# A fused sparse-attention and feed-forward kernel: the order of its side steps laid out anew

## The chip, the cores and the metric

The kernel runs on one core of a Trainium2 chip. The metric is device time in microseconds of one execution; a run is a whole execution, and the median of the runs shown is the time that counts. One further execution was profiled; its trace is what is read here. TensorE (PE, with its weight loads PEld) multiplies; VectorE (DVE), ScalarE (ACT) and GpSimd (POOL) do the rest; SyncE (SP) and ScalarE issue transfers. Each engine goes through its own list in order.

## What is computed

Attention for 8 batches, 8 heads, 576 tokens and 64 features a head: heads 0 to 3 see the last 32 tokens, heads 4 to 7 every 32nd token. Its output, 4608 tokens of 512 features, goes through a feed-forward layer with a hidden width of 2048.

```python
scores = scale * np.matmul(q, k.transpose(0, 1, 3, 2))
scores = np.where(masks[None, :, :, :], scores, -1000000000.0)
scores = scores - np.max(scores, axis=-1, keepdims=True)
attn = np.exp(scores)
attn = attn / (np.sum(attn, axis=-1, keepdims=True) + 1e-09)
attn_out = np.matmul(attn, v)
...
h = x @ w_in
g = np.where(pos, h, np.where(neg, 0.0, (h + beta) ** 2 / (4.0 * beta)))   # pos: h >= 1, neg: h <= -1
out = g @ w_out
```

## The kernel before

Tokens go through the feed-forward in columns of 512. The weights and activations are split into a high and a low half, and each product of 128x128 by 512 columns stands for one of three pairs of halves (high-high, high-low, low-high, in this order).

The first three chunks of 512 tokens are plain ("classic"): for each of 16 slices f of the hidden width, `up(c, f)` is 12 products into one of two PSUM banks, a gate on ScalarE and VectorE and a rounding to two halves follow, and `down` two slices later is 12 products, in two parts of six. The last 3072 tokens are three chunks of 1024, each computed with seven products of half-size blocks in place of eight: an up part of 56 units of six products (`up_block`, L988) and a down part of 28 units of 12 (`down_block`, L1039). A unit of the down part waits for two factors that SP fetches from DRAM into a ring of seven.

Beside the products stand the steps. All of them are written into tables, each with a position, and are issued in the order of positions. A position counts TensorE's chunks: six products are one position. The first chunk runs from -64 to 0 (slice f at -64 + 4f), the second from 0 to 64, the third from 64 to 128, and each of the large chunks takes 112 from 128 on. A step at a position is put into the program before the first TensorE chunk that is issued after that position: in the classic chunks there are three such places a slice (after `up`, between the two parts of `down`, after `down`), in the large chunks one after each unit. On TensorE this says where a step stands among the products; on another engine it says only which step comes before which. Semaphores do the rest.

```python
def until(t):
    while agenda and agenda[0][0] < t:
        _, _, do, what = agenda.pop(0)
        do(*what)
...
todo = [(GATE[c > 0], lambda: gate(c, f)), (ROUNDED[c > 0], lambda: pend.append((c, f, rounded(c, f))))]
if c or f > 1:
    gs = pend.pop(0)
    todo += [(2, lambda: down(*gs, (0, 1))), (3, lambda: down(*gs, (2, 3)))]
for at, do in sorted(todo, key=lambda x: x[0]):
    until(t + at)
    do()
until(t + 4)
```

The tables:

- `WORK[b]`: the attention of batch b, a letter and a unit 0 to 3 (units 0 and 1 are the local heads, 2 and 3 the strided). On TensorE: `s` scores (L544), `f` transposes (L671), `v` values and `V1` those of units 1 and 3 (L734). On VectorE: `m` mask (L604), `x` maximum (L630), `b` subtraction, `q` sum (L645), `w` reciprocal and product (L658), `t` transpose (L695), `l` low half (L810; it issues nothing for tokens from column 1536 on, which are kept whole). On ScalarE: `e` exponential, `p` sum plus epsilon, `h` copy of the values out of PSUM (L801). On POOL: `a` subtraction (L634); `r` is a reciprocal on VectorE (L657) and a product on POOL (L658). On SP: `j`, `J` a trip through DRAM, `Q`, `F`, `P` loads. Scores, transposes and values of the batches share two PSUM banks, so that a block waits until the step that reads the block before it out is done; from batch 5 on `s1`, `s3` and `v2` use two others.
- `CONV`: the conversion of weight slice f, half i (`E5.0` is the last step for up(0,5), `E5.1` for down(0,5)): `A`, `L` (L404, L408) and `D` (L425) on ScalarE, `B` (L412) and `E` (L429) on VectorE, `C` (L416) on POOL. `E` makes the low half.
- `SUMS`: sums of weight slices (POOL, ScalarE, VectorE, and a store on ScalarE's queue); `SHIP`: stores of weight slices to DRAM, on ScalarE's queue.
- `X_WORK`, `U_WORK`, `G_WORK`: sums, gates and splits of the large chunks; in `U_WORK`, `a111` adds a product's result to a block on VectorE (L964); in `G_WORK`, `r40` or `r30` takes a result out (L1020 on ScalarE, L1022 on VectorE) and SP stores it (L881).

The opening, up to the second slice of the first chunk, is an order of its own (`BEGIN`) and isn't touched.

Of the kernel before, what the change touches and what calls it, by code (L numbers as in the profile page):

```python
# [35 lines left out]
WORK = {1: [(-60.38, 's0'), (-55.74, 'm0'), (-55.4, 'x0'), (-52.6, 'a0'), (-51.93, 's1'), (-51.84, 'Q2 Q3'), (-51.74, 'e0 q0'),  # L36
# [196 lines left out]
def tile_sparse_attention_then_ffn(  # L233
# [843 lines left out]
    with tc.manual_schedule():  # L1077
# [25 lines left out]
        def sum_step(n, step):  # L1103
            s, half_ = SUMS[n][0]
            i, j = divmod(n, NP)
# [106 lines left out]
```

## Time and profile before

| | |
|---|---|
| median of 3 runs | 817.14 us (817.0 to 818.74) |
| profiled execution, its own time | 816.39 us |
| its span, first to last instruction | 814.6 us |
| TensorE busy | 803.3 us, 99% |
| VectorE busy | 572.1 us, 70% |
| ScalarE busy | 494.2 us, 61% |
| POOL busy | 242.3 us, 30% |
| granted TensorE clock | 1.0 of full speed throughout |

Busy times are unions of the instructions' spans. The share of TensorE leaves some 11 us of the span in which it does nothing, part of them before its first instruction and after its last.

### The profile page before, as it was taken

Reading aid. Unit: us, or ns where it says so; the run is one execution under the profiler, and the core shown is the slowest. Engines: PE = TensorE matmul, PEld = TensorE weight load, DVE = VectorE, ACT = ScalarE, POOL = GpSimd, SP = SyncE. Lnnn points to the kernel's source line nnn. Section 1 sums busy time; section 2 is a strip of 40 time slices with the busy share of each in tenths; the row PEclk is TensorE's granted clock in tenths of the full one; section 3 lists DMA queues with packets and bytes.
Section 4 is the critical chain, followed back from the end, with each engine's and each line's share of the span. In section 5 each row is a group of like instructions: output and inputs, shape, how many; then the busy total and the mean of one; then the engine's idle time right before and its main releaser. Section 6 shows DMA issues by size and latency. Waiting matters only on the chain.

```text
span 814.6 us, 17829 instructions
## 1 busy us (share of the span) xinstructions
PE 803.3 (99%) x6969; PEld 655.9 (81%) x6969; DVE 572.1 (70%) x845; ACT 494.2 (61%) x868; POOL 242.3 (30%) x229
## 2 busy tenths in 40 slices
PE   8999999999999999999999999999999999999997
PEld 6778888888878888887888888788888888888885
DVE  5998868767548547775698877765678733777672
ACT  5888855545355446577764464677745545885442
POOL 5454544873347520421134101230310000114000
PEclk9999999999999999999999999999999999999999
DMA  9935437788868775998888977897666776666764
GB/s 347 408 137 198 156 111 274 267 299 278 271 222 293 257 242 180 330 292 255 261 295 252 285 260 239 270 282 226 178 201 205 246 223 193 194 195 188 219 205 147
DMA packets 101795, 195.10 MB, mean 239 GB/s; under 512 B 17104, under 2 KB 32464, under 8 KB 99664
## 3 DMA queue, kind: packets, MB, share of 16 engines
q1 hardware_dynamic: 92496, 164.60, 63.6%
q10 hardware_dynamic: 9216, 29.36, 9.3%
q8 instruction: 55, 0.90, 0.4%
q14 instruction: 28, 0.23, 0.1%
HBM read 147.26 MB, written 46.66 MB: 238 GB/s over the span
## 4 chain that ended last, share of the span: by engine, by line
PE 95%; DMA 2%; issue 1%; DVE 0%; ACT 0%; POOL 0%; SPq 0%; ACTq 0%; POOLq 0%; DVEq 0%
PE yo L1039 16%; PE o L891 16%; PE y L988 16%; PE h L846 16%; PE zo L1039 8%; PE z L988 8%; PE x L988 4%; PE xo L1039 4%; PE xp L734 4%; PE sc L544 3%; DMA qk<-in_qk_s 2%; DMA v<-in_v_s 0%; PE tp L671 0%; POOL pr L634 0%; SPq L479 0%
## 5 line engine op out<-in xcount | busy, mean ns | idle before, releaser
L988 PE MATMUL y<-x,wr 128*128 128x512 f32 x576 | 141.6, 392 | 0.1
L846 PE MATMUL h<-xq,w 128*128 128x512 f32 x576 | 139.7, 391 | 0.5 <-DVE w L429 0.5
L1039 PE MATMUL yo<-hl,wr 128*128 128x512 f32 x576 | 133.1, 390 | 0.0
L891 PE MATMUL o<-gh,w 128*128 128x512 f32 x384 | 130.1, 399 | 0.0
L846 PEld LDWEIGHTS h<-xq,w 128*128 128x128 f32 x576 | 107.5, 188 | 23.6 <-DVE w L429 0.9
L988 PEld LDWEIGHTS y<-x,wr 128*128 128x128 f32 x576 | 107.1, 188 | 24.0 <-DVE gb L964 0.6
L1039 PEld LDWEIGHTS yo<-hl,wr 128*128 128x128 f32 x576 | 107.9, 188 | 22.6 <-DVE hl L943 0.3
L891 PEld LDWEIGHTS o<-gh,w 128*128 128x128 f32 x384 | 72.1, 188 | 16.1
L891 PE MATMUL o<-gl,w 128*128 128x512 f32 x192 | 75.0, 391 | 0.0
L988 PE MATMUL z<-x,wr 128*128 128x512 f32 x288 | 73.3, 390 | 0.0
L971 POOL TENSOR_TENSOR ga<-gb,ga 128x1024 f32<-128x1024 f32 x9 | 22.0, 2449 | 156.8 <-DVE ga L856 122.3
L634 POOL TENSOR_TENSOR pr<-pr,st 128x384 f32<-128x384 f32 (+3 forms) x22 | 29.2, 1326 | 132.8 <-DVE st L630 132.2
L1039 PE MATMUL zo<-hl,wr 128*128 128x512 f32 x288 | 66.1, 390 | 0.0
L943 DVE TENSOR_TENSOR hl<-ga,hl 128x1024 fp32r<-128x1024 f32 x36 | 50.0, 1391 | 21.2 <-ACT hl L942 20.2
L457 POOL TENSOR_TENSOR xs<-w 128x512 f32<-128x512 f32 x32 | 44.7, 1416 | 63.5 <-DMA ks<-xs 25.8
L988 PEld LDWEIGHTS z<-x,wr 128*128 128x128 f32 x288 | 54.0, 188 | 11.5 <-ACT gb L962 0.3
L1039 PEld LDWEIGHTS zo<-hl,wr 128*128 128x128 f32 x288 | 54.0, 188 | 11.2
L853 ACT ACTIVATE tmp<-tmp 128x512 f32<-128x512 f32 x96 | 60.7, 633 | 3.0
L942 ACT CAST hl<-ga 128x1024 fp32r<-128x1024 f32 x36 | 37.8, 1053 | 39.2 <-PE yo L1039 15.7
L856 DVE SCALAR_TENSOR_TENSOR h<-h,u 128x512 f32<-128x512 f32 x47 | 32.7, 696 | 39.4 <-ACT u L853 39.0
L459 POOL TENSOR_TENSOR xs<-xs 128x256 f32<-128x256 f32 x64 | 52.3, 818 | 5.0
L850 ACT ACTIVATE u<-h,half 128x512 f32<-128x512 f32 x48 | 33.0, 688 | 32.5 <-PE h L846 26.9
(118 smaller groups left out, 1320.0 us busy)
## 6 DMA issues: line engine op xcount, KB each, us to landing
wr<-ks SPq DMA_DIRECT2D x192, 256.0 KB, 3.8
wr<-kq SPq DMA_DIRECT2D x144, 256.0 KB, 3.5
ks<-xs ACTq DMA_DIRECT2D x16, 1024.0 KB, 5.0
raw<-in_w SPq DMA_DIRECT2D x30, 512.0 KB, 9.5
kq<-w ACTq DMA_DIRECT2D x48, 256.0 KB, 3.7
qk<-in_qk_s SPq DMA_DIRECT2D x16, 604.0 KB, 5.9
qk<-in_qk_l SPq DMA_DIRECT2D x16, 576.0 KB, 5.7
v<-in_v_l SPq DMA_DIRECT2D x21, 384.0 KB, 5.7
```

The lines of the kernel that those rows point to most:

```text
L457: nc.gpsimd.tensor_tensor(out=b[:, :, f] if i else b[:, f], in0=hi, in1=lo, op=ALU.add)
L459: nc.gpsimd.tensor_tensor(out=st[:, to, HF:], in0=st[:, x, HF:], in1=st[:, y, HF:], op=op)
L734: nc.tensor.matmul(xp[p][j * D:(j + 1) * D, n], loaded[b, local, b0 + n][keys, j], qs, start=True, stop=True)
L846: nc.tensor.matmul(o_ps[c, f], wt[f][:, 0, h, x, e:e + P], xq[c][:, y, cc], start=first and n == 0, stop=last and n == len(todo) - 1)
L850: nc.scalar.activation(u, h, AF.Relu, bias=half, scale=0.5)
L853: nc.scalar.activation(u, u, AF.Square)
L856: nc.vector.scalar_tensor_tensor(out=to, in0=h, scalar=1.0, in1=u, op0=ALU.max, op1=ALU.min)
L891: nc.tensor.matmul(o_ps[c][d], wt[f][:, 1, h, x, e:e + P], gs[y], start=f == 0 and n == 0, stop=f == NF - 1 and n == 2)
L942: nc.scalar.copy(t[:, 0], src)
L943: nc.vector.tensor_tensor(out=t[:, 1], in0=src, in1=t[:, 0].bitcast(F32), op=ALU.subtract)
L988: nc.tensor.matmul(banks_of[s, q, j], w_[:, a, c * P:(c + 1) * P], xc[m][:, b, c], start=m in (1, 2, 5) and c + i == 0, stop=c == 1 and i ...
L1039: nc.tensor.matmul(to, w_[jj][:, a, d * P:(d + 1) * P], t[:, b, jj], start=m in (1, 2, 5) and k + jj + q == 0, stop=k == NP // 2 - 1 and j ...
```

## The change

All seven tables are replaced; nothing else is. The old and the new tables hold the same steps on the same engines, at other positions, but for five entries that are left out (`l1` of batch 2, `l0` to `l3` of batch 3). Entries that stood together at one position ('Q2 Q3', 'e0 q0') stand alone now. Positions up to -56 are the same. Over all kinds of steps the mean of the moves lies between some 4 positions earlier and 2.3 later; single steps move by up to 57 positions (a `SHIP`), most by one to three. The core of the diff, with the lines that hold the steps named below:

```diff
--- before.py
+++ after.py
@@ -33,200 +33,202 @@
...
-WORK = {1: [(-60.38, 's0'), (-55.74, 'm0'), (-55.4, 'x0'), (-52.6, 'a0'), (-51.93, 's1'), (-51.84, 'Q2 Q3'), (-51.74, 'e0 q0'),
-     (-51.61, 'p0'), (-51.49, 'm1'), (-51.2, 'x1'), (-51.12, 'a1'), (-50.21, 'r0'), (-47.65, 'e1'), (-47.64, 'q1'),
-     (-47.42, 'p1'), (-46.21, 'w1'), (-43.77, 'f0'), (-43.76, 'd0'), (-39.64, 's2'), (-39.4, 'm2 x2'), (-39.15, 'a2'),
-     (-35.94, 'v0'), (-35.84, 'F2'), (-35.81, 'e2'), (-35.73, 'q2'), (-35.57, 'h0 l0'), (-35.39, 'p2'), (-35.14, 'w2'),
...
-     (28.85, 'k3 r3'), (28.89, 'j2'), (29.15, 'J2'), (37.36, 'v2'), (37.46, 't3'), (37.87, 'h2'), (38.0, 'l2'),
-     (38.81, 'j3'), (41.17, 'J3'), (41.32, 'F4'), (44.62, 'V1'), (45.06, 'h1'), (45.32, 'l1'), (46.1, 'h3'),
-     (46.78, 'l3')],
- 3: [(26.83, 'Q0 Q1'), (29.08, 's0'), (37.27, 'm0'), (37.65, 'x0'), (37.85, 'b0'), (39.59, 'e0'), (40.48, 's1'),
...
-     (59.22, 'F2'), (59.61, 'h0'), (59.9, 'l0'), (59.93, 'x3'), (60.67, 't2'), (61.19, 'j2'), (61.5, 'F3 a3'),
...
-     (71.38, 'h2'), (72.41, 'F4'), (72.61, 'j3'), (73.19, 'l2'), (75.79, 'J3'), (82.43, 'V1'), (82.61, 'h1'),
-     (83.08, 'l1'), (83.16, 'h3'), (89.51, 'l3')],
...
-     (159.74, 'j3'), (163.55, 'v2'), (163.58, 'v0'), (163.89, 'F2'), (163.96, 'h0'), (164.19, 'F4'), (165.84, 'J3'),
...
-     (206.47, 't3'), (206.57, 'j3'), (209.86, 'F2'), (210.31, 'F4'), (210.71, 'h0'), (214.02, 'J3'), (218.14, 'v2'),
-     (218.76, 'V1'), (219.91, 'h2'), (219.92, 'h3'), (222.97, 'h1')],
...
-     (250.0, 's2'), (250.07, 's3'), (250.6, 'F3'), (250.87, 'm2'), (251.05, 'x2'), (251.16, 'p1'), (251.38, 'w1'),
...
-SUMS = [((0, 0), 30.03, 34.27, 34.91, 37.39), ((1, 1), 64.0, 67.03, 67.68, 74.53), ((0, 0), 16.76, 22.19, 23.74, 27.21),
...
- ((0, 0), 9.8, 15.48, 15.83, 16.18), ((1, 0), 73.17, 74.86, 75.67, 80.37), ((1, 1), 120.48, 122.48, 123.07, 124.52),
...
-X_WORK = {0: [(115.78, 2), (116.82, -7), (116.86, 1), (117.06, -6), (118.89, -4), (121.4, 7), (121.65, 4), (124.38, -5), (127.97, 5),
-     (128.22, 3), (128.79, 6)],
...
+WORK = {1: [(-60.38, 's0'), (-55.91, 'm0'), (-55.76, 'x0'), (-53.32, 'a0'), (-51.97, 'e0'), (-51.96, 'q0'), (-51.47, 's1'),
+     (-51.36, 'm1'), (-51.34, 'p0'), (-50.76, 'x1'), (-50.67, 'a1'), (-48.41, 'Q2'), (-47.84, 'r0'), (-44.93, 'e1'),
+     (-44.33, 'q1'), (-42.98, 'f0'), (-42.41, 'd0'), (-42.39, 'Q3'), (-42.29, 'p1'), (-41.64, 'w1'), (-38.33, 's2'),
+     (-37.48, 'm2'), (-37.45, 'x2'), (-35.84, 'a2'), (-35.7, 'v0'), (-35.68, 'h0'), (-35.6, 'e2'), (-35.37, 'F2'),
...
+     (36.92, 'J2'), (37.23, 'j3'), (37.38, 'v2'), (37.5, 'F4'), (38.57, 'J3'), (41.16, 'h2'), (41.35, 'l2'),
+     (44.18, 'V1'), (44.27, 'h1'), (45.93, 'h3'), (46.32, 'l3')],
+ 3: [(20.68, 'Q0'), (20.81, 'Q1'), (33.83, 's0'), (34.87, 'm0'), (34.99, 'x0'), (35.17, 'b0'), (39.66, 'e0'),
...
+     (161.1, 'j3'), (163.15, 'v2'), (163.36, 'h2'), (163.65, 'v0'), (163.95, 'F2'), (164.03, 'F4'), (164.28, 'h0'),
...
+     (208.37, 'r3'), (208.82, 'h0'), (209.24, 'F4'), (209.6, 't3'), (211.22, 'j3'), (212.22, 'v2'), (213.76, 'J3'),
+     (217.43, 'h2'), (219.15, 'V1'), (219.45, 'h3'), (230.78, 'h1')],
...
+     (255.23, 'w1'), (255.27, 't1'), (255.28, 'j1'), (255.3, 'a2'), (255.38, 'm3'), (256.09, 'e2'), (257.07, 'x3'),
...
+SUMS = [((0, 0), 30.98, 34.91, 35.07, 35.23), ((1, 1), 68.97, 69.39, 69.64, 74.86), ((0, 0), 20.69, 22.48, 22.88, 24.84),
...
+ ((0, 0), 7.28, 16.02, 16.64, 17.61), ((1, 0), 75.37, 76.25, 76.45, 78.18), ((1, 1), 115.03, 120.59, 122.35, 122.43),
...
+X_WORK = {0: [(101.78, 2), (110.78, 1), (118.17, -7), (118.33, -6), (121.1, -4), (123.64, 6), (123.89, 7), (129.32, -5), (129.48, 5),
+     (130.33, 3), (130.78, 4)],
...
 CONV = [(-63.99, 'L0.1'), (-63.97, 'A0.1 B0.1'), (-63.52, 'A1.1'), (-63.03, 'C0.1'), (-62.58, 'A3.0'), (-62.43, 'D0.1'),
...
- (-51.25, 'D3.1'), (-50.93, 'A4.1'), (-50.92, 'D5.0'), (-50.23, 'E3.1'), (-50.1, 'L4.1'), (-48.56, 'A6.0'),
- (-48.52, 'A5.1'), (-48.35, 'E5.0'), (-48.16, 'B4.1'), (-47.95, 'B6.0'), (-47.76, 'L6.0'), (-47.49, 'C4.1'),
- (-47.41, 'C6.0'), (-47.32, 'D4.1'), (-47.0, 'D6.0'), (-46.02, 'B5.1'), (-45.33, 'E6.0'), (-45.2, 'A7.0'),
...
- (-40.36, 'B7.1'), (-40.04, 'B8.0'), (-40.0, 'E7.0'), (-39.97, 'C7.1'), (-39.68, 'A6.1'), (-39.52, 'B6.1'),
- (-39.43, 'C8.0'), (-39.38, 'L6.1 C6.1'), (-39.09, 'D8.0'), (-38.69, 'A9.0'), (-38.65, 'L8.1'), (-38.44, 'E5.1'),
...
-     (456.33, 's43'), (461.13, 'r31'), (462.11, 'r41'), (462.46, 'r40'), (462.86, 'r30')]}
...
-     (249.85, 'n110'), (251.85, 'c111'), (252.05, 'a111'), (253.16, 'a011'), (254.14, 'n000'), (254.8, 'a001'),
...
-SHIP = [[1.27, 12.82, 7.42, 20.53, 13.61, 18.54, 30.97, 29.74, 34.32, 31.23, 40.56, 58.58, 43.6, 47.29, 57.58, 63.72],
- [67.18, 66.59, 57.74, 75.26, 81.54, 83.67, 104.23, 102.07, 98.47, 104.8, 100.58, 117.35, 100.49, 112.74, 129.16, 115.04]]
...
+ (-55.32, 'A4.1'), (-55.2, 'L5.0'), (-55.18, 'C4.0'), (-55.11, 'D2.1'), (-55.04, 'A5.0'), (-53.89, 'B5.0'),
...
+ (-51.62, 'C3.1'), (-50.95, 'C5.0'), (-50.81, 'L7.0'), (-49.52, 'D5.0'), (-49.22, 'L4.1'), (-49.17, 'E5.0'),
+ (-49.12, 'A5.1'), (-48.6, 'B5.1'), (-48.43, 'D3.1'), (-48.27, 'E3.1'), (-47.37, 'B4.1'), (-47.08, 'A6.0'),
+ (-46.92, 'B6.0'), (-46.8, 'L6.0'), (-46.78, 'C6.0'), (-46.52, 'A6.1'), (-46.47, 'C4.1'), (-45.48, 'L7.1'),
...
+ (-40.1, 'D7.0'), (-40.04, 'B6.1'), (-40.01, 'E7.0'), (-39.22, 'C6.1'), (-39.0, 'D6.1'), (-38.87, 'D5.1'),
+ (-38.57, 'C8.0'), (-37.88, 'D8.0'), (-36.66, 'E5.1'), (-36.58, 'E6.1'), (-36.5, 'E8.0'), (-36.47, 'C7.1'),
...
+     (458.33, 'r30'), (459.48, 's42'), (460.23, 's43'), (463.1, 'r40'), (463.12, 'r41')]}
...
+     (250.14, 'a001'), (250.83, 'f100'), (250.84, 'n100'), (251.23, 'c111'), (251.56, 'a111'), (251.84, 'f111'),
...
+SHIP = [[3.6, 1.13, -1.06, 29.51, 16.74, 37.99, 36.33, 16.76, -22.29, 32.1, 44.04, 93.57, 29.6, 34.85, 70.16, 53.52],
+ [80.62, 41.72, 52.33, 89.6, 79.44, 84.1, 109.2, 107.22, 99.77, 113.42, 99.29, 122.61, 66.19, 118.4, 121.29, 96.06]]
...
```

## Rows read from the trace of the kernel before

**Rows 1.** The page: busy us (share of the span) xinstructions; the chain by engine.
```profile
PE 803.3 (99%) x6969; PEld 655.9 (81%) x6969; DVE 572.1 (70%) x845; ACT 494.2 (61%) x868; POOL 242.3 (30%) x229
...
PE 95%; DMA 2%; issue 1%; DVE 0%; ACT 0%; POOL 0%; SPq 0%; ACTq 0%; POOLq 0%; DVEq 0%
```

**Rows 2.** The chain in order of time: start us, us, what.
```profile
754.97 21.76 PE yo L1039 x96
```

**Rows 3.** ScalarE's timeline, 38.5 to 45.5 us: start, us, instruction.
```profile
38.80 0.69 ACT L425 CAST w<-raw 128x512 fp32r<-128x512 f32 x1 [0.22 <-POOL raw L416]
...
42.97 0.66 ACT L850 ACTIVATE u<-h,half 128x512 f32<-128x512 f32 x1
```

**Rows 4.** TensorE's timeline at three blocks of values, and the next product.
```profile
177.66 1.28 PE L734 MATMUL xp<-pT,v 54*64 54x64 f32 x48
178.87 0.50 PE L891 MATMUL o<-gh,w 128*128 128x512 f32 x1
...
231.85 0.93 PE L734 MATMUL xp<-pT,v 54*64 54x64 f32 x48
232.71 1.66 PE L846 MATMUL h<-xq,w 128*128 128x512 f32 x6
...
391.89 1.51 PE L734 MATMUL xp<-pT,v 64*64 64x32 f32 x88
393.34 0.96 PE L988 MATMUL y<-x,wr 128*128 128x512 f32 x3
...
465.81 2.30 PE L734 MATMUL xp<-pT,v 54*64 54x64 f32 x136
468.04 1.20 PE L1039 MATMUL zo<-hl,wr 128*128 128x512 f32 x4
```

**Rows 5.** SP's timeline at the end.
```profile
810.92 0.41 SPq L881 DMA_DIRECT2D out<-kept  x1
```

**Rows 6.** Timelines around 517 and at 53.7 us; line L412 (min/median/max ns).
```profile
516.86 1.52 PE L988 MATMUL z<-x,wr 128*128 128x512 f32 x6
518.51 1.66 PE L988 MATMUL y<-x,wr 128*128 128x512 f32 x6
...
516.22 1.64 DVE L658 TENSOR_TENSOR pr<-pr,st 128x384 f32<-128x384 f32 x1
...
516.17 1.27 POOL L634 TENSOR_TENSOR pr<-pr,st 128x648 f32<-128x648 f32 x1 [2.46 <-DVE st L630]
...
53.69 0.56 DVE L658 TENSOR_TENSOR pr<-pr,st 128x384 f32<-128x384 f32 x1
...
L412 DVE TENSOR_SCALAR raw<-raw x34: 290/420/1694, 15.3 to 108.4; 128x512 uint32<-128x512 uint32 x30, 128x256 uint32<-128x256 uint32 x4
```

**Rows 7.** Timelines of TensorE, VectorE and POOL, 47 to 53 us.
```profile
48.12 0.67 PE L846 MATMUL h<-xq,w 128*128 128x512 f32 x2
49.28 2.57 PE L846 MATMUL h<-xq,w 128*128 128x512 f32 x10 [0.50 <-DVE w L429]
...
51.47 0.80 PEld L671 LDWEIGHTS tp<-ident,pr 128*128 128x128 f32 x6
...
48.47 0.22 DVE L657 RECIPROCAL st<-st 128x12 f32<-128x12 f32 x1
...
48.83 1.73 POOL L658 TENSOR_TENSOR pr<-pr,st 128x768 f32<-128x768 f32 x1 [1.33 <-DVE st L657]
```

**Rows 8.** Timelines of VectorE and TensorE, 63 to 68 us.
```profile
64.28 0.68 DVE L429 TENSOR_TENSOR w<-raw,w 128x512 fp32r<-128x512 f32 x1
...
66.31 0.39 PE L891 MATMUL o<-gl,w 128*128 128x512 f32 x1
```

**Rows 9.** TensorE's timeline, 377 to 382 us; the page's queue of instructions (packets, MB).
```profile
377.88 2.06 PE L734 MATMUL xp<-pT,v 54*64 54x64 f32 x126
381.67 0.53 PE L734 MATMUL xp<-pT,v 64*64 64x32 f32 x18 [1.72 <-issue]
...
q8 instruction: 55, 0.90, 0.4%
```

More of the change, by code (lines that the diff above doesn't have):

```diff
@@ L34 @@
 """
-WORK = {1: [(-60.38, 's0'), (-55.74, 'm0'), (-55.4, 'x0'), (-52.6, 'a0'), (-51.93, 's1'), (-51.84, 'Q2 Q3'), (-51.74, 'e0 q0'),
[60 rows of a table removed]
-SUMS = [((0, 0), 30.03, 34.27, 34.91, 37.39), ((1, 1), 64.0, 67.03, 67.68, 74.53), ((0, 0), 16.76, 22.19, 23.74, 27.21),
[5 rows of a table removed]
-X_WORK = {0: [(115.78, 2), (116.82, -7), (116.86, 1), (117.06, -6), (118.89, -4), (121.4, 7), (121.65, 4), (124.38, -5), (127.97, 5),
-     (128.22, 3), (128.79, 6)],
- 1: [(209.29, 2), (219.97, -7), (227.35, 7), (227.46, 1), (233.2, -6), (233.37, -5), (234.98, 5), (236.4, -4), (236.56, 3),
-     (237.47, 6), (242.51, 4)],
- 2: [(299.32, 1), (314.83, -7), (323.8, 7), (337.11, -6), (338.91, 6), (343.56, 2), (346.68, 3), (349.06, -4), (352.84, -5),
-     (353.14, 5), (355.46, 4)]}
+WORK = {1: [(-60.38, 's0'), (-55.91, 'm0'), (-55.76, 'x0'), (-53.32, 'a0'), (-51.97, 'e0'), (-51.96, 'q0'), (-51.47, 's1'),
[62 rows of a table added]
+SUMS = [((0, 0), 30.98, 34.91, 35.07, 35.23), ((1, 1), 68.97, 69.39, 69.64, 74.86), ((0, 0), 20.69, 22.48, 22.88, 24.84),
[5 rows of a table added]
+X_WORK = {0: [(101.78, 2), (110.78, 1), (118.17, -7), (118.33, -6), (121.1, -4), (123.64, 6), (123.89, 7), (129.32, -5), (129.48, 5),
+     (130.33, 3), (130.78, 4)],
+ 1: [(205.79, 2), (224.98, -7), (227.85, 1), (230.24, 3), (230.48, -6), (231.26, 7), (233.63, -5), (234.83, 5), (236.33, 6),
+     (243.8, -4), (246.02, 4)],
+ 2: [(313.53, -7), (314.04, 7), (321.14, 1), (324.67, -6), (334.3, 3), (339.28, 6), (340.36, -5), (347.71, 2), (348.2, 5),
+     (355.6, -4), (358.13, 4)]}
 CONV = [(-63.99, 'L0.1'), (-63.97, 'A0.1 B0.1'), (-63.52, 'A1.1'), (-63.03, 'C0.1'), (-62.58, 'A3.0'), (-62.43, 'D0.1'),
@@ L114 @@
  (-59.28, 'A2.1'), (-59.01, 'D3.0'), (-58.67, 'L2.1'), (-58.57, 'C1.1'), (-57.92, 'D1.1'), (-57.44, 'E3.0'),
[26 rows of a table removed]
-G_WORK = {0: [(163.63, 's11'), (168.49, 's10'), (174.23, 't61'), (187.39, 's12'), (187.57, 't62'), (187.87, 's13'), (190.2, 's20'),
[26 rows of a table removed]
-U_WORK = {0: [(129.08, 'c000'), (129.42, 'a000'), (131.86, 'c010'), (132.04, 'c110'), (133.41, 'c001'), (134.41, 'a110'),
[59 rows of a table removed]
-SHIP = [[1.27, 12.82, 7.42, 20.53, 13.61, 18.54, 30.97, 29.74, 34.32, 31.23, 40.56, 58.58, 43.6, 47.29, 57.58, 63.72],
- [67.18, 66.59, 57.74, 75.26, 81.54, 83.67, 104.23, 102.07, 98.47, 104.8, 100.58, 117.35, 100.49, 112.74, 129.16, 115.04]]
[26 rows of a table added]
+G_WORK = {0: [(164.39, 's11'), (172.16, 't61'), (173.92, 's10'), (187.71, 's12'), (187.99, 't62'), (188.06, 's13'), (188.53, 's20'),
[26 rows of a table added]
+U_WORK = {0: [(129.53, 'c000'), (129.8, 'a000'), (131.21, 'c110'), (131.78, 'c010'), (132.97, 'a110'), (133.25, 'f000'),
[59 rows of a table added]
+SHIP = [[3.6, 1.13, -1.06, 29.51, 16.74, 37.99, 36.33, 16.76, -22.29, 32.1, 44.04, 93.57, 29.6, 34.85, 70.16, 53.52],
+ [80.62, 41.72, 52.33, 89.6, 79.44, 84.1, 109.2, 107.22, 99.77, 113.42, 99.29, 122.61, 66.19, 118.4, 121.29, 96.06]]
 @with_exitstack
```

313 rows, old and new, of tables (CONV, G_WORK, SUMS, U_WORK) are left out of this document.

## The prediction

> **What bounds the kernel now.** First the page's busy times and its chain [rows 1]: TensorE is busy 99% of the span, and 95% of the chain that ended last is its own work. Then the chain piece by piece [rows 2]: 96 products take 21.76 us, 0.227 us each, back to back. A position, as the tables count, is six products, 1.36 us. So the time is TensorE's instruction list plus the few places where TensorE waits, and a new order of the steps can only win these places or add new ones. Third, ScalarE's timeline in the opening: from 38.80 to 42.97 seven steps run without a break [rows 3]. There the steps have no room; later they have.
>
> **The sum is made against the profiled execution**: span 814.6 us, its own time 816.39, so 1.8 us lie around the span. The median of the runs is 817.14, 0.75 above that execution; I add the sum to the median. About 0.2%, 1.6 us, is what a measurement of this kernel can tell from no change.
>
> **What is the same.** Every step that issues an instruction stands in both tables, 1,235 of them, on the same engine and queue; TensorE's products keep their order, and gate and rounding their offsets. The five steps that go (`l1` of batch 2, `l0` to `l3` of batch 3) issue nothing: those tokens lie past column 1536, where there is no low half. Splitting 'Q2 Q3' into two entries costs nothing by itself: SP goes through its list in order and waits for semaphores alone. Cost of all this: 0. It is the order that must be costed, where it touches a row.
>
> **Part 1, TensorE's list.** Between the products stand blocks of scores and values. Counting the chunks into which the old and the new positions fall, 45 blocks become 46: `v2` and `V1` of batch 6 (218.14 and 218.76, one block) part to 212.22 and 219.15. The joint block of 136 takes 2.23 us from its first instruction to the next product; blocks of the same two sizes alone take 0.86 and 1.45 [rows 4]: +0.08. For a second entry and restart I allow 0.2, less than one product's pitch. **+0.28**, bounds 0.08 and 0.35.
>
> **Part 2, the tail.** Behind the last products three stores follow on SP; the third (of kept, from `r30` at 462.86) is issued at 810.92 for 0.41 us [rows 5]. `r30` moves to 458.33, ahead of the last two units of products, so its addition and its store fall under 5 us of products, and the last store is issued 0.41 earlier. **-0.41**, bounds -0.41 and 0 (if the second store lands last anyway).
>
> **Part 3, two waits that go.** `v2` of batch 2 starts at 177.66 and the next product comes 1.21 us later; the equal block at 231.85 needs 0.86 [rows 4]. `m0` of batch 3, at 37.27 for a block at 38, still read the two banks; now it stands at 34.87, three positions ahead. **-0.35**, bounds -0.35 and 0. At 518.51 TensorE waits for `a111` of chunk 1: six products from 516.86 would end at 518.22, so 0.29. `a111` stands on VectorE behind `w1` of batch 7, a step of 128x384 that took 1.64 us there and 0.56 elsewhere [rows 6]. Now `a111` (251.56) comes before `w1` (255.23). **-0.29**, bounds -0.29 and 0.
>
> **Part 4, the full stretch.** TensorE's one long wait for a conversion is in up(0,5): two products at 48.12, the third, the first to read the low half, at 49.28 instead of 48.57, when `E5.0` is done on VectorE [rows 7]. There `E5.0` was behind `E3.1` and `r0`'s reciprocal; now both come after it, -0.8 by durations (0.68 as of `E5.1` [rows 8], 0.22, less overlap). But ScalarE takes `A4.1` in ahead of gate(0,3), at the 0.60 of its seven steps [rows 3]; so that gate, the rounding behind it, and up(0,5) itself, which needs the bank that the rounding reads, come 0.6 later. Together **0**, bounds -0.2 and +0.2.
>
> What is late next is `r0`. Its reciprocal ended at 48.69, POOL's step ran from 48.83 to 50.56, and the transposes of `f0` began loading at 51.47 [rows 7]: 0.9 us to spare. Now `E5.0` and `B5.1` (0.42 by the median of its line [rows 6]) stand before it, some 0.95 with the overlap of the rows, and 0.6 comes from gate(0,3). 50.56 + 1.55 = 52.1 against 51.47: **+0.65**, bounds 0.05 (ScalarE catches up) and 0.65. Behind POOL's step are queued `C6.0` and `C4.1`; their units come three positions or more later.
>
> Then `E5.1`, for down(0,5). It ended at 64.96; the second product of that unit runs at 66.31, the third, which reads its low half, 0.23 later [rows 8]: 1.58 us to spare. It moves from -38.44 to -36.66, 1.78 positions or 2.42 us: 0.84 late, less the 0.65 by which TensorE itself is late by then: **+0.2**, bounds 0 and 0.84. The other E steps keep over three positions ahead of their units and wait in the same queue; once TensorE is late, all have that much more. So these lags don't add up: the largest counts.
>
> **Part 5, the instruction wait.** The longest wait is no step's: `v2` and `v0` of batch 5 run 126 of their 144 small products from 377.88, then TensorE stands 1.72 us for "issue" [rows 9]. 126 products with their weight loads are 252 instructions; queue q8 brought 55 packets of instructions in the run, for twice 6,969 of them 253 each [rows 1, 9]. The block outran one packet. The two steps keep their order and their chunk (before 164), and TensorE's list ahead of them is the same but for its separate waits, so the packet ends near the same spot: **0**, bounds -1.72 and 0. The Trainium skill (Runtime: NRT & Kernel Launch, Instruction fetch mechanics) has blocks of 256 instructions, fetched while the one before runs, and a crossing mostly hidden; the count agrees, the 1.72 us don't, and by "hidden" the sum would be 1.72 lower.
>
> **Sum:** 0.28 - 0.41 - 0.35 - 0.29 + 0 + 0.65 + 0.2 + 0 = +0.08. 817.14 + 0.08 = 817.2 us. All low ends together give -2.84, 814.3; all high ends +2.04, 819.2.
>
> **Rivals.**
> *Faster: the instruction wait goes.* If the separate waits ahead of the block rise by some fifteen instructions, the request for the next packet comes 15 x 0.113 = 1.7 us earlier (a product and its load share 0.227) and the wait is hidden: 817.2 - 1.72 = 815.5, and with `r0` on its low end 814.9. For it: few instructions decide. Against: nothing in the tables aims at it, and as many fewer leave it where it is. 0.24.
>
> *Slower: VectorE held by POOL in the full stretch.* At 516.22 VectorE's step of 0.56 us took 1.64 beside a POOL step from 516.17 to 517.44, and L412, 0.42 by its median, reaches 1.69 [rows 6]. One such hold, 1.27 us, just ahead of `E5.1` goes on to TensorE; the new order moves the B steps against POOL's `C7.1`, `C6.1`, `a2` and `r0` between -50 and -32. `E5.1` would then be 0.84 + 1.27 - 0.65 = 1.46 late in place of 0.2: 818.5; with one more hold on a step with nothing to spare 819.7. It decides from the point where VectorE falls 1.5 us behind what the rows show. Against: the run before has such holds too, at other places. The Trainium skill (SBUF — State Buffer, Who interferes with whom) says that only one pair of ports contends, VectorE's and GpSimd's, by an exclusive lock; 517.44 + 0.56 = 518.0 against the measured end of 517.86 agrees. 0.26.
>
> *No difference to speak of* is the forecast: TensorE's list decides, and the small waits trade. 0.50.
>
> **Numbers.** Likeliest 817.2, its own range 815.5 to 818.8. Eight in ten: from 814.6 (instruction wait gone, `r0` hidden, and a little of the rest) to 819.8 (two holds). Faster by over 0.2% 0.24, within it 0.50, slower 0.26.
>
> **What would show it.** TensorE busy 99% again. No store of kept after the last copy. The block of batch 2's `v2` at 0.86 us. No wait for chunk 1's `a111`. A wait for POOL before the transposes near 51.5, of 0.1 to 0.65. One wait for "issue" of about 1.7 in the joint block of batch 5. The forecast would be wrong if TensorE's waits for VectorE or ScalarE between 45 and 110 us sum to over 2, or if it waits for a weight fetch or a sum in the units past 327 us, where I costed two places alone.

## The result

The changed kernel takes 829.58 us (median of 6 runs, 827.16 to 831.11) against 818.33 us (817.0 to 822.81) of the kernel before on the same chip: a ratio of 1.0124, 95% interval 1.0093 to 1.0156. It is slower by 11 us, where 817.2 with a range up to 819.8 was forecast. The profiled execution has a span of 825.4 us, 10.8 more than before.

The page's busy times and its chain, of the changed kernel, beside [rows 1]:

```profile
PE 808.7 (98%) x6969; PEld 656.8 (80%) x6969; DVE 575.4 (70%) x845; ACT 494.1 (60%) x868; POOL 241.3 (29%) x229
...
PE 77%; ACT 12%; DVE 4%; DMA 2%; POOL 2%; issue 2%; ACTq 0%; SPq 0%; DVEq 0%; POOLq 0%
```

The instructions are the same. TensorE's own work was 95% of the chain and is 77%: the chain now leaves TensorE and runs through other engines, so their steps set the time at more places. (That share is of the chain, and is not time lost.) TensorE's busy time rose by 5.4 us with the same list, and its idle time by the other 5.4 (16.7 of the span instead of 11.3).

**Where the time went.** The products of 128x512 come in the same order in both kernels, so the start of the same product in both traces gives the lag. The points stand where both have the same score and value blocks behind them.

| stretch | product: before, after (us) | lag |
|---|---|---|
| first chunk, slice 14 | 110.02, 110.35 | +0.3 |
| behind the scores of batch 2 | 122.09, 128.69 | +6.6 |
| second chunk | 154.31, 161.86 | +7.6 |
| end of the third chunk | 305.91, 314.15 | +8.2 |
| first large chunk begins | 332.40, 341.93 | +9.5 |
| behind a late weight fetch | 362.73, 374.07 | +11.3 |
| behind the block of batch 5 | 382.13, 391.48 | +9.4 |
| last product's end | 809.36, 821.39 | +12.0 |
| span | 814.6, 825.4 | +10.8 |

One place takes 6.3 of it. The new waits of TensorE, from its list of waits (engine, line, for what: total us, times, longest):

```profile
PE sc L546 <- DMA qk<-in_qk_l: 4.4, 2, 4.1
PE y L990 <- DMA wr<-ks: 1.2, 1, 1.2
...
PE xp L736 <- ACT xs L803: 0.8, 2, 0.5
PE sc L546 <- DVE xq L812: 0.7, 1, 0.7
PE y L990 <- ACT gab L964: 0.7, 1, 0.7
PE o L893 <- ACT gh L876: 0.6, 1, 0.6
```

And the largest of them, in the timelines of TensorE, VectorE and SP of the changed kernel, with the stretches around it (busy time of each engine, granted clock, transfers):

```profile
118.74 0.72 PE L546 MATMUL sc<-qk 64*32 64x64 f32 x48
123.59 0.72 PE L546 MATMUL sc<-qk 64*32 64x64 f32 x48 [4.13 <-DMA qk<-in_qk_l]
124.25 4.61 PE L848 MATMUL h<-xq,w 128*128 128x512 f32 x12
...
118.12 1.75 DVE L431 TENSOR_TENSOR w<-raw,w 128x256 fp32r<-128x256 f32 x2
...
119.90 0.33 SPq L481 DMA_DIRECT2D qk<-in_qk_l  x1
...
119.00:123.60 4.60, 0.47 (x45) 0.30 (x22) 2.17 (x4) 1.04 (x1) 2.82 (x4) 1.00 0.56 186
123.60:128.00 4.40, 4.40 (x58) 3.49 (x58) 2.94 (x4) 0.00 (x0) 0.00 (x0) 0.61 0.89 303
```

Read from below: SP issues `Q1` of batch 2 (the queries and keys of its second pair of heads) at 119.90, right when `E15.1` ends on VectorE (118.12 + 1.75 = 119.87). The load lands 3.7 us later; half the scores have waited 4.13 us for it. Then the granted clock is 0.61 of full speed on average and twelve products take 4.44 us instead of 2.72: another 1.72. In the kernel before the same two steps were, with the scores that run through:

```profile
120.99 1.17 PE L544 MATMUL sc<-qk 64*32 64x64 f32 x96
...
108.86 2.67 DVE L429 TENSOR_TENSOR w<-raw,w 128x256 fp32r<-128x256 f32 x5 [0.18 <-ACT w L425]
...
110.92 0.96 SPq L479 DMA_DIRECT2D qk<-in_qk_l  x2
```

`E15.1` ended at 111.53, and the second of the two loads went out at 111.55. The last weight piece and `Q1` share a buffer (both come from the pool `qk_p`, which has two). `E15.1` is the last reader of the piece, so it sets when `Q1` can start. The change moves it from -7.81 to -3.16, behind the gate of slice 15: 8.3 us later. It also moves the scores (`s0` of batch 2) from 0.1 to -0.5, ahead of the twelve products of up(0,15) instead of behind them.

### The profile page after: what moved, and what is told of

It reads as the page before. It is cut to its first block, busy times and chain, and to the rows that moved or that the text cites. A ratio compares the mean times of both kernels' runs of the same rounds, so it can differ in the third digit from the quotient of the medians.

```text
span 825.4 us, 17835 instructions
## 1 busy us (share of the span) xinstructions
PE 808.7 (98%) x6969; PEld 656.8 (80%) x6969; DVE 575.4 (70%) x845; ACT 494.1 (60%) x868; POOL 241.3 (29%) x229
## 4 chain that ended last, share of the span: by engine, by line
PE 77%; ACT 12%; DVE 4%; DMA 2%; POOL 2%; issue 2%; ACTq 0%; SPq 0%; DVEq 0%; POOLq 0%
PE yo L1041 15%; PE o L893 12%; PE y L990 12%; PE h L848 12%; PE zo L1041 8%; PE z L990 6%; PE xo L1041 4%; PE xp L736 3%; ACT tmp L852 3%; PE x L990 3%; ACT tmp L855 3%; PE sc L546 2%; ACT raw L406 1%; DMA qk<-in_qk_l 1%; POOL xs L461 1%
## 5 line engine op out<-in xcount | busy, mean ns | idle before, releaser
L848 PE MATMUL h<-xq,w 128*128 128x512 f32 x576 | 141.9, 395 | 0.0
L1041 PEld LDWEIGHTS zo<-hl,wr 128*128 128x128 f32 x288 | 54.0, 188 | 11.3
L636 POOL TENSOR_TENSOR pr<-pr,st 128x384 f32<-128x384 f32 (+3 forms) x22 | 27.4, 1247 | 97.8 <-DVE st L632 97.8
```

Of the source, the lines that this page charges most:

```text
L636: eng.tensor_tensor(out=pr, in0=pr, in1=st[:, 0].unsqueeze(2).broadcast_to(list(pr.shape)), op=ALU.add)
L848: nc.tensor.matmul(o_ps[c, f], wt[f][:, 0, h, x, e:e + P], xq[c][:, y, cc], start=first and n == 0, stop=last and n == len(todo) - 1)
L1041: nc.tensor.matmul(to, w_[jj][:, a, d * P:(d + 1) * P], t[:, b, jj], start=m in (1, 2, 5) and k + jj + q == 0, stop=k == NP // 2 - 1 and j ...
```

## The experiments

Times are medians; ratios are against the kernel before in the same session, with 95% intervals. The medians of before there lie between 819.8 and 820.8.

| kernel | us | ratio | interval |
|---|---|---|---|
| E15.1 late | 819.69 | 0.9992 | 0.9963 to 1.0020 |
| E15.1 late, scores early | 828.59 | 1.0107 | 1.0066 to 1.0148 |
| ten steps back | 830.03 | 1.0126 | 1.0089 to 1.0163 |
| twelve steps back | 824.21 | 1.0048 | 1.0032 to 1.0064 |
| zeros in the wait | 828.85 | 1.0101 | 1.0055 to 1.0147 |
| old, then new | 822.04 | 1.0027 | 1.0000 to 1.0053 |
| new, then old | 828.94 | 1.0103 | 1.0050 to 1.0157 |
| mended new | 818.51 | 0.9994 | 0.9973 to 1.0016 |
| sum put later | 826.93 | 1.0097 | 1.0066 to 1.0129 |
| new in the middle | 815.58 | 0.9929 | 0.9904 to 0.9954 |
| more zeros | 821.11 | 1.0008 | 0.9983 to 1.0033 |
| three moves | 817.39 | 0.9965 | 0.9944 to 0.9987 |
| four moves | 814.31 | 0.9938 | 0.9918 to 0.9958 |
| far split | 815.61 | 0.9942 | 0.9917 to 0.9966 |
| v0 first | 816.48 | 0.9943 | 0.9925 to 0.9962 |

**The late load, made and unmade.** *E15.1 late* puts the cause alone into the kernel before, two positions in `CONV`:

```diff
- (-7.92, 'D15.1'), (-7.81, 'E15.1')]
+ (-3.31, 'D15.1'), (-3.16, 'E15.1')]
```

> Buffer theory (the load Q1 of batch 2 goes into the buffer that the last weight piece sits in, and E15.1 is the last to read it): E15.1 comes behind the gate of slice 15, ends near 118, Q1 is issued right behind it and lands near 122, so the scores of batch 2, at 121 in the kernel before, wait 0.5 to 2 us; 0.5 to 2 slower than before, and up to 1.8 more if the clock falls behind that wait as it did in the changed kernel. Rival (the 4.3 us come from the crowded transfer queue or from the new order of the loads on SP): no change, within 0.3.

The load of its trace goes out at 118.91, where `E15.1` ends (118.88), and the scores wait:

```profile
118.91 0.33 SPq L479 DMA_DIRECT2D qk<-in_qk_l  x1
...
122.69 0.72 PE L544 MATMUL sc<-qk 64*32 64x64 f32 x48 [1.24 <-DMA qk<-in_qk_l]
```

1.24 us, as the buffer theory has it, and no slow products behind. In time it can't be told from before. *E15.1 late, scores early* moves one more step, `s0` of batch 2, to where the change has it:

```diff
- 2: [(-13.48, 'F0'), (-11.61, 'Q0 Q1'), (-6.26, 'F1'), (0.1, 's0'), (0.19, 'm0'), (0.24, 'x0'), (2.24, 'b0'),
+ 2: [(-13.48, 'F0'), (-11.61, 'Q0 Q1'), (-6.26, 'F1'), (-0.5, 's0'), (0.19, 'm0'), (0.24, 'x0'), (2.24, 'b0'),
```

> Buffer theory: the same late Q1, but the scores of batch 2 now start near 118.5, so TensorE waits 3.5 to 4.5 us and the products behind run at the lower clock for about 4 us (1.8 us lost): 5 to 6.5 slower than before, as in the changed kernel. Rival (queue or order of loads): within 0.5 of before.

8.6 us slower than before, where 5 to 6.5 was expected: three steps make most of the changed kernel's loss. Of the lag in its trace 6.5 us arise at this place, and 2.2 in the opening, which the edit doesn't touch (granted clock 0.51 from 17.2 to 24.2 us). The wait splits in another way than expected: 1.84 for "issue", 0.44 for the low half of batch 1 (`l3`, which stands behind `E15.1` on VectorE here) and 1.33 for the load, and the low clock follows:

```profile
122.33 0.27 PE L544 MATMUL sc<-qk 64*32 64x64 f32 x2 [1.84 <-issue]
123.04 0.92 PE L544 MATMUL sc<-qk 64*32 64x64 f32 x46 [0.44 <-DVE xq L810]
125.30 0.97 PE L544 MATMUL sc<-qk 64*32 64x64 f32 x48 [1.33 <-DMA qk<-in_qk_l]
126.20 4.75 PE L846 MATMUL h<-xq,w 128*128 128x512 f32 x12
```

*Ten steps back* takes the changed kernel and returns `D` and `E` of 14.0 and 14.1 and all six steps of 15.1 to their old positions:

```diff
- (-11.37, 'D14.0'), (-11.18, 'E14.0'), (-7.62, 'D14.1'), (-7.37, 'E14.1'), (-6.91, 'L15.1'),
- (-6.78, 'A15.1'), (-6.3, 'B15.1'), (-6.03, 'C15.1'), (-3.31, 'D15.1'), (-3.16, 'E15.1')
+ (-14.56, 'D14.0'), (-13.85, 'E14.0'), (-8.24, 'D14.1'), (-8.13, 'E14.1'), (-9.55, 'L15.1'),
+ (-11.47, 'A15.1'), (-9.8, 'B15.1'), (-8.08, 'C15.1'), (-7.92, 'D15.1'), (-7.81, 'E15.1')
```

> Buffer theory: with the ten steps back at their old positions Q1 is issued near 112.5 and lands by 118, the wait near 119 and the low clock behind it go: 5 to 6.3 faster than the changed kernel, so 823.3 to 824.6, still 6 to 7 slower than before. Rival (another step late at the same place takes over): less than 2.5 faster than the changed kernel, above 827.

It gained nothing, as its rival has it. The wait at 119 was gone, but the ten steps now stood ahead of `c3` of batch 1 on ScalarE (still at -7.78) and themselves waited for the weight piece, so the values of batch 1 waited instead, and slow products followed again:

```profile
113.63 1.61 PE L736 MATMUL xp<-pT,v 54*64 54x64 f32 x40 [3.96 <-ACT pT L683]
```

*Twelve steps back* returns `f3` and `c3` as well (-8.09 to -11.72, -7.78 to -11.69).

> The changed kernel with the ten conversion steps back and, this time, the transposes f3 of batch 1 and their copy c3 as well, which the ten had pushed behind the load of the last weight piece. Buffer theory: the wait near 110 goes too, Q1 lands by 118, nothing waits near 119: 5 to 6.5 faster than the changed kernel, 4 to 6 slower than before. Rival: again a wait of over 2 us between 105 and 130.

824.21, 5.4 less than the changed kernel (6.2 by the ratios), as expected; nothing waits for the load any more, one wait of 1.42 for slice 15 remains ahead of up(0,15).

*Zeros in the wait* asks about the slow products alone: the changed kernel, with TensorE kept at work while it waits.

```diff
- (-0.5, 's0')
+ (-0.51, 'Zs0:38'), (-0.5, 's0')
```

> The changed kernel with 38 products of zeros (256 columns, 0.11 us each) just ahead of the scores that wait. Clock theory: the wait for the load still ends near 123.6, but TensorE was not idle, the granted clock stays at 1.0 and the ten products behind take 0.227 us each instead of 0.427: 1.7 to 2 faster than the changed kernel. Rival (they are slow from the transfers or their operands): still 0.427 each, no gain.

```profile
118.38 4.39 PE L531 MATMUL sc<-zeros 128*128 128x256 bf16 x38
122.71 1.40 PE L546 MATMUL sc<-qk 64*32 64x64 f32 x96
124.04 3.01 PE L848 MATMUL h<-xq,w 128*128 128x512 f32 x12
...
123.60:128.00 4.40, 4.40 (x65) 3.65 (x46) 2.93 (x4) 0.87 (x2) 0.00 (x0) 1.00 0.80 286
```

The clock stays at 1.00, and the product behind the twelve starts at 126.89 instead of 128.69, 1.8 us earlier. So the slow products were TensorE's lower level after standing idle, not the transfers. The whole kernel gained 1.9 by the ratios (1.0124 to 1.0101), which their intervals don't tell from nothing; its trace has a wait for instructions of 1.19 at the block of batch 5 besides.

**The rest, by halves.** *Old, then new* gives every step that stood below position 0 its old position and all others the new one; *new, then old* is its mirror image.

> Every step that stood below position 0 keeps its old position, all others the new one (not below 0). If the loss sits in the first chunk's order (late Q1, the lower clock behind it, and 0.7 us of small waits from 60 to 110), 6 to 7.5 us of the changed kernel's loss go, and what is left is the later waits less the gains: 2 to 5.5 slower than before. Rival (the late steps only pass the wait on, as when ten steps alone were moved back): 8 or more slower than before.

> The mirror image: new positions below 0, old ones from there on. If the loss sits in the first chunk: 5 to 8 slower than before, with a wait for the load of batch 2 near 119 of 3 to 4.5 us (its scores are back at 0.1, one product group later) and slow products behind it. Rival (it takes the new order behind 0 as well): under 3 slower.

The first is 2.2 slower than before, the second 9.1, more than the 5 to 8 expected: the first chunk carries the loss. In the second, the scores wait 4.11 for `Q1` again (`s0` of batch 2 stands at -0.5 in it, not at 0.1 as the expectation says), and other scores of batch 2 wait 2.17 for a low half near 162. What the first has left sits at five places, each a step late in its own engine's order. Its trace at one of them, the scores of batch 2 that wait for `l0`, behind a sum of weight slices on VectorE:

```profile
154.52 1.38 PE L538 MATMUL sc<-qk 64*64 64x54 f32 x40 [1.38 <-DVE xq L804]
...
155.00:160.00 5.00, 5.00 (x49) 4.11 (x50) 4.07 (x8) 1.28 (x3) 4.76 (x7) 0.66 0.95 305
```

1.38 us of waiting, and the clock at 0.66 for five more. *Mended new* moves one step or two at each of the five:

```diff
- SUMS, fourth entry: 18.67, 18.84 (round, rest)
+ SUMS, fourth entry: 20.4, 20.45
- WORK[4]: (116.24, 'h2'); WORK[5]: (144.53, 'J0'); X_WORK[0]: (123.64, 6), (123.89, 7)
+ WORK[4]: (110.0, 'h2'); WORK[5]: (141.5, 'J0'); X_WORK[0]: (127.0, 6), (127.2, 7)
- U_WORK[2] as after
+ U_WORK[2] as before, and with it s10 and s11 of G_WORK[2]
```

> The kernel with the old order below position 0 and the new one behind it, with the later waits mended one by one: the sums of slice 3 behind l0 of batch 2, h2 of batch 4 at 110.0, two splits of the first large chunk behind the last gate, J0 of batch 5 at 141.5, the old U_WORK of the last chunk. If each wait has the cause read off the trace (the step named, late in its engine's own order), all five go: 1.45 us and the 1.7 of low clock behind it near 154, 0.8 near 308, 1.3 near 327, 1.3 near 369, 1.6 between 690 and 732, together 7 to 8 less than that kernel, 3 to 6 faster than before. Rival (each mended place passes its wait on): within 1.5 of the kernel it mends.

All five waits are gone from its trace, but the kernel gained 3.5 (2.7 by the ratios), not 7 to 8: the old `U_WORK[2]` beside the new tables made others at the start of the last chunk, 1.16 us the longest:

```profile
660.95 1.66 PE L982 MATMUL z<-x,wr 128*128 128x512 f32 x6 [1.16 <-ACT last L1014]
```

*New in the middle* keeps that mended order from 0 to 340 only and the old one on both sides, with `r30` and `r40` early.

> The mended kernel with the new order from position 0 to 340 alone; below and above it the old one, with r30 and r40 early. If the 2.8 us of waits at the start of the last large chunk (661 to 668) came from old and new tables mixed there, they go: 2.5 to 4 faster than the mended kernel, 3.5 to 5.5 faster than before, about as fast as with four moves. Rival (the new middle has waits of its own that cost what the moves win): within 1.5 of the mended kernel.

815.58, 2.9 less than mended new; those waits are gone.

*Sum put later* (old, then new, with the four steps of one sum of slices 8 to 12 positions later) tests whether VectorE is held by POOL. The additions of the next sum, which go to the same place, now stand ahead of this sum's rounding: they overwrite it before it is used, so this kernel works without the right sum. They also no longer wait for its store, and so the additions that ran beside the splits come 13 us earlier (309.43 instead of 322.84), not later.

> The same kernel with one sum of weight slices (POOL, two additions of 128x512 that ran from 323 to 327 beside the split on VectorE) put 12 positions later, and nothing else. If VectorE was held by POOL there: the split of 128x1024 takes 1.2 to 1.4 us instead of 2.3, the last gate comes 1.0 earlier and the wait of 1.28 us in front of the last products of the classic part falls under 0.4. Rival (the two splits stand ahead of the gate, that alone makes it late): the wait stays over 0.8.

Old, then new (VectorE, POOL), and below it this kernel (VectorE, POOL):

```profile
322.26 3.46 DVE L937 TENSOR_TENSOR x<-xs,x 128x1024 fp32r<-128x1024 f32 x2 [0.26 <-ACT x L936]
...
322.84 4.03 POOL L451 TENSOR_TENSOR xs<-w 128x512 f32<-128x512 f32 x2 [13.04 <-DMA ks<-xs]
```

```profile
318.78 2.36 DVE L937 TENSOR_TENSOR x<-xs,x 128x1024 fp32r<-128x1024 f32 x2 [0.26 <-ACT x L936]
...
313.03 4.97 POOL L453 TENSOR_TENSOR xs<-xs 128x256 f32<-128x256 f32 x4
339.75 1.47 POOL L628 TENSOR_TENSOR pr<-pr,st 128x768 f32<-128x768 f32 x1 [21.75 <-DVE st L624]
```

Two splits took 3.46 (1.23 and 2.32) beside POOL's additions and 2.36 with POOL idle. In the first kernel ScalarE's part of the last gate was done at 324.42, and VectorE's began only at 325.65, behind the splits; 1.1 less would have brought it to 324.6 and left, as an estimate, 0.2 of TensorE's wait of 1.28. In this kernel the wait vanished wholly, but ScalarE's steps came earlier too, so the run alone doesn't part the two. The Trainium skill (SBUF — State Buffer, Who interferes with whom) says that a VectorE step with two operands in SBUF contends with a POOL step that reads SBUF, and that this contention is an exclusive lock. This pair agrees: the split that began ahead of POOL's first addition took 1.23, the one that began beside it 2.32. As a whole the kernel is slower: the sum's last steps now stand ahead of the large chunk's, ScalarE waits 2.91 for one of them on VectorE near 335, and TensorE 1.84 for ScalarE, with the low clock behind.

**The wait for instructions and the named moves.** *More zeros* adds ten products to the opening of the kernel before (`Zs0:17` to `Zs0:22`, `Zf0:9` to `Zf0:14`), to shift where a packet of instructions ends.

> Instruction theory (the 1.72 us before the last 18 small products of batch 5 depend only on where the packet of instructions ends): ten more products of zeros in the opening's waits, 20 instructions, bring the request 2.3 us earlier relative to the block; the wait goes, 1.4 to 1.7 faster than before, less up to 0.4 for the opening. Rival (the wait comes from the block's length alone, or from the transfers around it): the wait stays, 0 to 0.5 slower.

The wait stayed, 1.95 after 116 of the 144 small products. The packet boundary had moved as meant, but the packet came no earlier against the block. *Four moves* changes the kernel before in four places:

```diff
- WORK[3]: (37.27, 'm0'); WORK[7]: (251.38, 'w1'); G_WORK[2]: (462.11, 'r41'), (462.46, 'r40'), (462.86, 'r30')
+ WORK[3]: (34.87, 'm0'); WORK[7]: (252.4, 'w1'); G_WORK[2]: (462.11, 'r41'), (462.1, 'r40'), (458.33, 'r30')
- WORK[5]: (163.58, 'v0'), (163.89, 'F2'), (163.96, 'h0'), (164.19, 'F4')
+ WORK[5]: (164.5, 'v0'), (164.55, 'F2'), (164.6, 'h0'), (164.58, 'F4')
```

> The kernel before with four local moves, each read in its own place. Values of batch 5 in two blocks, one unit apart: the block no longer outruns its instructions, 1.72 gone, 0.2 for the second block (rival: the wait goes with the packet to another place and stays 1 us or more). Results r30 and r40 earlier: from the last product to the end 4.0 instead of 5.25 (rival: 4.85, the third store alone). Mask of batch 3 ahead: the values of batch 2 at 0.86 instead of 1.21. Product w1 of batch 7 behind a111: 0.29 gone near 518. Together 3 to 3.6 faster than before; with the rivals 1.2.

*Three moves* is the same without the move of `v0`.

> The kernel with four moves, less the parting of batch 5's values into two blocks. If the parting does nothing for the instructions' wait (it was there in the one profile with it): as fast as with four, 3 to 5 faster than before. If it does: slower by 1 to 2 than with four moves. By the three places alone 1.3 + 0.35 + 0.3 = 2 faster than before.

Four moves are 5.1 faster by ratio (0.9938 of 820), more than the 3 to 3.6 expected, and three 2.9. The two intervals overlap, so it isn't shown that parting the block is worth the 2 us between them. The profiled execution of four moves still had 1.50 of the wait in the second block and the low clock behind it; it took 817.35 at a granted clock of 0.997, while eight of the ten executions took 813.2 to 815.5 at 0.999 or 1.000 (of three moves, four of eleven reached 0.999). That fits a wait which was missing in most of them. *Far split* puts `v0` at 166.0 (F2, F4, `h0` behind it), three units of products behind `v2`, and also `E3.1` behind `E5.0` (-50.23 to -48.27):

> The kernel before with r30 and r40 earlier, the mask of batch 3 and the product w1 of batch 7 moved, the last conversion E3.1 put behind E5.0, and the values of batch 5 in two blocks that now lie two units more apart than in the kernel with four moves. Packet theory (TensorE resumes 1.4 us after the end of the packet's transfer, and in the profile of four moves the second block came before that): with 3.6 us between the blocks neither waits, and no slow products follow: 4 to 6 faster than before, and as fast as with four moves or up to 1.5 faster. Rival (the wait follows the block wherever it goes): a wait of over 1 us in one of the two blocks again.

There neither block waits, but V1 of batch 5 does, for the loads that moved along:

```profile
377.10 0.93 PE L734 MATMUL xp<-pT,v 54*64 54x64 f32 x48
...
382.26 1.60 PE L734 MATMUL xp<-pT,v 64*64 64x32 f32 x96
...
390.65 1.89 PE L734 MATMUL xp<-pT,v 64*64 64x32 f32 x88 [1.12 <-DMA v<-in_v_l]
```

*v0 first* is far split with `v0` (160.0), F2, F4 and `h0` ahead of `v2` instead.

> As the last kernel with the parted values of batch 5, but v0 now goes ahead of v2 by three units, and the two loads of values that wait for it (F2, F4) come with it, so that V1 of batch 5 no longer waits for them (1.12 us there). Packet theory: blocks of 96 and 48 some 4 us apart wait for no instructions, no slow products follow: 0.6 to 1.3 faster than that kernel, 5 to 6.5 faster than before. Rival (the packet's wait or the load's comes back at another block): no faster than that kernel.

Neither wait is left in its trace, and the stretch from 355 to 394 us (in times of the kernel before) took 1.2 less than in far split, as expected; still the whole kernel is no faster than far split. The trace shows what it lost elsewhere in this execution: the opening ran at a granted clock of 0.51 from 16.6 to 23.5 us, where no step was moved. The four best kernels (four moves, far split, new in the middle, v0 first) can't be told apart; each is 0.6 to 0.7% faster than before, and so faster than either kernel of the change.

## Why the prediction was wrong, by its steps

**The step that failed** is in part 4: the E steps were costed for the products that read their result ("the other E steps keep over three positions ahead of their units"), and the largest lag counted. `E15.1` keeps ahead of its unit. It was not asked what else waits for it: the buffer that it reads, and through it a load on SP and the scores of batch 2. No row of the load was read. Part 1 did the same with the blocks: it counted them, but gave the move of these scores by twelve products no cost. Each move alone leaves room: E15.1 late waits 1.24 us and can't be told from before in time, and in twelve steps back the scores still stand at -0.5 and don't wait. Both together cost 8.6. In the changed kernel they made 6.3 us of lag, 1.7 of them the clock, which no term of the sum had.

**A second step** is the forecast's own condition, "units past 327 us, where I costed two places alone". Between 306 and 363 us the lag grows by 3.1: the last gate of the third chunk, behind two splits that ran beside POOL, and a weight fetch, 1.19, that stood on SP behind `J0` (four issues in 4.51 us) and a spread of batch 5. In the last chunk the new `U_WORK[2]` adds 1.9 (the lag is 10.1 at 596 and 12.0 at 737), three copies out of PSUM behind gates. Mended new shows these causes, in that each wait went with its step; in the last chunk only the table as a whole was put back.

By the lags, the terms that the sum had came to some -3 us together (+0.3, -1.3, -0.65, +0.6 and -2.0 for parts 1 to 5), and the places without a term to the other +14, of 10.8 in all.

**Part 1** was right, in size too: the two blocks take 0.85 and 1.45 where the joint one took 2.23 [rows 4], and the lag is 9.62 ahead of both and 9.93 behind them, +0.31 against the forecast's +0.28:

```profile
467.28 0.93 PE L736 MATMUL xp<-pT,v 54*64 54x64 f32 x48
468.13 3.02 PE L1041 MATMUL yo<-hl,wr 128*128 128x512 f32 x12
...
476.52 1.52 PE L736 MATMUL xp<-pT,v 64*64 64x32 f32 x88
477.97 1.20 PE L1041 MATMUL zo<-hl,wr 128*128 128x512 f32 x4
```

**Part 2** was right in sign and mis-sized: -0.41 forecast, -1.27 measured (last product's end to the end of the span 5.25 before, 3.98 after). The missed part is that `r40` now comes ahead of `r41`, so one copy and one store run under the last products too; with the same swap four moves gives 3.88.

**Part 3** held: the values of batch 2 start at 185.18 and the next product at 186.04, 0.86; there is no wait for `a111` of the second large chunk, and the lag falls by 0.30 there (forecast 0.29). In three moves the lag falls by 0.35 behind the values of batch 2, as forecast.

**Part 4's own terms** came out small, as forecast: the wait for `E5.0` went (twelve products run through from 47.90), the transposes of `f0` then wait for POOL, whose step ends at 51.05, some 0.5 us, and nothing waits for `E5.1`. The lag goes from -0.24 at 47 us to +0.33 at 110: 0.57 against the forecast's 0.85.

**Part 5** was wrong on the good side, by luck: the wait for instructions is gone in this trace (389.25, the block of 144 in 2.23 to the next product), 2.0 won. Its reason, that the wait stays where the packet's end stays, does not hold: in E15.1 late, scores early, the packet ends after the same 126 products and the wait is 0.32. Nor does the rival's: the separate waits ahead of the block went from 114 to 107, where it asked for more, and twenty more instructions did not remove it.

**The rivals.** The faster one's gain came, by another way than it named, and was buried. The slower one named a mechanism that is there, at the wrong place and price: not the full stretch, but the end of the third chunk, about 1 us.

## What to carry to other kernels

When a step moves in a table of positions, list what it frees as well as what it makes: the next load into the buffer that it reads may be the tightest user of it. Cost a wait of over a microsecond on TensorE with and without slow products behind it. And make the moves that a row supports, each in its own place: three of them, and a block parted in two, made this kernel 0.6% faster, the whole new order made it 1.2% slower.

## What the runs showed of the hardware

**The clock after a wait.** A wait cost up to some 2.2 times its length (1.38 us and 1.7 of the lower clock in old, then new). After 4.13 us of waiting, the granted clock was 0.61 of full speed over the next 4.4 us, so most of them at 1.2 instead of 2.4 GHz, with 0.427 us a product instead of 0.227; after 1.38 us in old, then new 0.66 over 5 us. Behind the waits for instructions in E15.1 late, four moves and three moves (1.44, 1.50 and 1.78 us) it was 0.50 for 3.4 us, in three moves so:

```profile
381.54 0.47 PE L734 MATMUL xp<-pT,v 64*64 64x32 f32 x17 [1.78 <-issue]
...
382.90:386.30 3.40, 3.40 (x10) 2.63 (x9) 0.27 (x1) 1.93 (x4) 0.00 (x0) 0.50 0.24 70
```

But after 1.24 us in E15.1 late and after the 1.72 in the kernel before [rows 9] it stayed at 1.00, so from the wait's length alone it can't be told. The Trainium skill (TensorE: Matmul & The Clock Gate, Part 1) has the engine at half rate after it was idle; the zeros in the wait agree.

The same clock goes in part with the spread of one kernel's times. In the experiments' sessions the kernel before ran 93 times, 815.6 to 826.6 us. The 24 executions with a mean granted clock of 0.999 or more took 818.1 in the median, the 19 with 0.995 or less 822.7. The profiled one (816.39, clock 1.00) is of the first kind.

**The packet of instructions.** In nine traces with a wait in the block of batch 5 (0.32 to 1.96 us), TensorE went on 1.33 to 1.59 us after the packet's transfer ended on queue q8: among them 380.22 to 381.67 before, 382.28 to 383.73 in E15.1 late, 388.47 to 389.80 in E15.1 late, scores early. What differs is when the transfer begins against the block: 1.41 us behind its first product before, 0.93 ahead of it in the changed kernel, where the packet landed at 389.25 and there was no wait. E15.1 late, scores early has the block and the order around it as before, and there it began 0.35 ahead; so the tables alone don't set it, and the 2.0 us that the changed kernel won are those of one execution. What makes the packet late stays open. Transfers alone don't tell the two apart: they took 0.99 of the engines' time from 378 to 381 before, with the long wait, and 1.01 from 385.0 to 388.5 in E15.1 late, scores early, with the short one.
